# One attention-and-experts kernel: two gathers, one set of transposes and four row tiles change their place

## The chip, the cores and the metric

The kernel runs on one NeuronCore of a Trainium2 chip, as one program with one launch. The metric is device time in microseconds (us). Before the change the median of three runs is 446.9 us (446.38 to 448.73).

The engines that matter here: TensorE (PE in the profile, its weight loads PEld), VectorE (DVE), ScalarE (ACT), GpSimd (POOL) and SyncE (SP), which issues most of the transfers. Each engine works through its own instructions in order; semaphores tie them together.

## The reference, cut to what matters

Two blocks follow each other. The first is a linear attention with decay over 4 sequences (B), 8 heads of 64 (H, D) and 768 positions, cut in blocks of 64:

```python
intra = np.einsum('bhic,bhjc->bhij', qb, kb) * Dmask[None]      # scores, decayed and causal
intra = np.einsum('bhij,bhjd->bhid', intra, vb)
inter = np.einsum('bhid,bhde->bhie', qb * lam_pow[None], kv_state)
out[:, :, sl] = intra + inter
kv_state = lam_block * kv_state + np.einsum('bhsd,bhse->bhde', kb * rev_pow[None], vb)
```

Its output, 3072 rows of 512 numbers, goes through a mixture of 8 experts. Each row takes the expert with the highest logit, or keeps the expert of the row before it where a local gate says so:

```python
fresh_e = int(np.argmax(logits[b, s]))
e = fresh_e if s == 0 or local_gate[b, s] < 0.5 else prev_e
h = np.maximum(x[b, s] @ w1[e], 0.0)
out[b, s] = p[e] * (h @ w2[e])
```

## The kernel before

**Attention, 24 steps.** The kernel takes blocks of 128 positions instead of 64. A step `s` is one block of 128 positions of one sequence (`ORDER`, line 33): the four sequences take turns, so steps 0 to 3 are the first blocks of the four, 4 to 7 the second blocks, and so on. Steps 20 to 23 are the last blocks, which update no state. In one step:

- `loaded` brings queries, keys and values of a step in by SP (1 MB; 0.75 MB for the last four), five steps ahead.
- `prepare` lets POOL multiply the queries by the decay powers (`qd`, line 178, "decayed queries") and the keys by theirs (`kd`, line 181), three steps ahead.
- `scores(s + 1)` is the product of keys and queries in PSUM (`ps`, lines 201 and 209), and DVE multiplies it by the decay mask into `sm` (line 213). For steps in `WIDE` it is 8 matmuls of 128 columns and all positions; otherwise it is 16 matmuls on quarters of the array, which leave the half above the diagonal out. (A float32 matmul is two records in the trace, so these are x16 and x32 there.) There is one pair of `ps` tiles, so the next scores wait until DVE has read the last.
- `from_state` (line 236) is the product of state and decayed queries, `mix` (line 249) adds scores times values into the same PSUM tile `po`, and ACT copies the result into `xc` (line 252). `xc` holds one step of each sequence.
- `update` (line 263) brings the state forward; DVE adds it (line 266).

**Rows out.** The output of a step is held turned, and must be turned back into rows for `x_dram`, from where the experts gather rows. This happens in one of two ways. `rows_of` uses four PE transposes (line 273), an ACT copy (line 278) and one transfer of 256 KB, which ACT's queue issues (line 282). For steps in `TURNED`, `turned_rows` uses one DVE transpose (line 294), and after the last step of a group of four, `group_out` sends four transfers by SP (line 302). `TURNED[r]` is the step in which row tile `r` is turned. Before, these are steps 0 to 11 (mostly one step later) and 20 to 22.

**Routing, between the steps.** `gates` and `logits` take the logits of four steps. `extras` (line 793) spreads the routing of the first 12 tiles of rows over steps 9 to 22, most of it on DVE: `fresh_experts`, `along_sequences`, `experts_of`, `ranks`, `first_tiles`, `tokens_to_first_tiles`, `brought`, `by_slots`. It ends at (19, 1) with `gidx` (line 650), the row indices. At (20, 0) POOL issues the first two gathers, `ahead(0, 0)` and `ahead(1, 1)` (line 725), of 128 rows each, into `xgt[0]` and `xgt[1]`.

**The first expert tile.** `first_turned` (lines 732 to 735) transposes `xgt[0]` on PE into `pr` and lets DVE copy it to `xtt[0]`. The first product of the experts, `hidden(0, 0, 0)` (line 753), reads it directly after step 23.

**Experts.** 5 whole tiles are worked through while the rest of the routing is done, then pairs of tiles, whole tiles and half tiles as the counts need. Weights come by SP (lines 701 to 709, 831 to 837), 2 MB each.

**Order.** PE, DVE, SP and POOL follow the order in which the program is written (`manual_schedule`, line 807); only ACT is ordered by the scheduler. Ahead of the change, within step `s`, the order is: `loaded`, `prepare(s + 3)`, weight loads, `scores(s + 1)`, `from_state(s)`, logits, extras, gates, `mix(s)`, `update(s)`, `first_turned` in step 23, rows out, late extras.

Of the kernel before, what the change touches and what calls it, by code (L numbers as in the profile page):

```python
# [38 lines left out]
PARTS = [(0, 8), (8, NA), (NA, NT)]  # L39
LOADS = 6  # L40
QUARTERS = [16, 17, 18, 19]
WIDE = [3, 4, 5, 7, 9, 11]
TURNED = {**{r: r + 1 for r in range(3 * B)}, 11: 13, 20: 22, 21: 23, 22: 23}
WARM = 10
KA = -(-(NA * P - E * (P - 1)) // P)

# [19 lines left out]
def kernel(  # L66
# [120 lines left out]
    def scores(s):  # L187
        x = inp[s]
        qt = x[:, 0].rearrange("p (a i) -> p a i", i=P)
        kt = x[:, 1].rearrange("p (a i) -> p a i", i=P)  # L190
        if s == 1:
            ps = [t.rearrange("p (a i) -> p a i", i=P) for t in (pl, pr)]
        else:
            ps = pss


        if s in WIDE:
            for a in range(A):
                for u in range(2):
                    rows = slice(DH * u, DH * u + DH)  # L200
                    nc.tensor.matmul(ps[u][:, a], lhsT=kt[rows, a], rhs=qt[rows, a],
                                     start=True, stop=True, skip_group_check=True)
        for a in range(A if s not in WIDE else 0):
            for j in range(2):
                first = DH * j if s > 1 else 0
                half = slice(DH * (j ^ a & 1), DH * (j ^ a & 1) + DH)
                for u in range(2):
                    rows = slice(DH * u, DH * u + DH)
                    nc.tensor.matmul(ps[u][half, a, first:], lhsT=kt[rows, a, half], rhs=qt[rows, a, first:],  # L209
                                     start=True, stop=True, skip_group_check=True)  # L210
        sm = sms[s] = att.tile([P, 2, A, P], F32, name="sm")
        for u in range(2):
            nc.vector.tensor_tensor(sm[:, u], ps[u], mask[:, u], ALU.mult)  # L213
# [14 lines left out]
    def from_state(s):  # L228
        b, c = ORDER[s]
        head = heads[s] = place_of(s)  # L230
        if c:
            kv, qd = kvs[b], qds.pop(s)
            for a in range(A):
                for u in range(2):
                    rows = slice(DH * u, DH * u + DH)
                    nc.tensor.matmul(head(a, u), lhsT=kv[rows, a], rhs=qd[rows, a],  # L236
                                     start=(a < 2), stop=False, skip_group_check=True)
            if c + 1 < NC:
                for a in range(A):
                    nc.scalar.mul(kv[:, a], kv[:, a], lamq[:, a, P - 1:P])  # L240
# [491 lines left out]
    def first_turned():  # L732
        for d in range(DT):
            nc.tensor.transpose(pr[:, P * d:P * d + P], xgt[0][:, P * d:P * d + P], ident)
        nc.vector.tensor_copy(xtt[0].rearrange("p d i -> p (d i)"), pr)  # L735
# [67 lines left out]
    def extra_work(s, k):  # L803
        if (s, k) in extras:
            extras[s, k]()

    with tc.manual_schedule(engines={PE, DVE, SP, POOL}):

        warm = pg.tile([P, A, P], F32, name="pk0")
        for _ in range(WARM):  # L810
            nc.tensor.matmul(warm[:, 0], lhsT=ident, rhs=ident, start=True, stop=True)
        masks_of_lam()
        nc.gpsimd.memset(wgt, 0.0)
        constants_1()

        for s in range(LOADS - 1):
            inp[s] = load.tile([P, 4, DM], F32, name="inp")
        for s, half in ((0, 0), (1, 0), (0, 1), (1, 1), *((s, half) for s in range(2, LOADS - 1) for half in range(2))):
            nc.sync.dma_start(out=inp[s][:, 2 * half:2 * half + 2], in_=qkv[s][:, 2 * half:2 * half + 2])
        for s in range(3):  # L820
            prepare(s)
        scores(0)
        nc.sync.dma_start(out=wgt[:, :, :E + 1], in_=wg)
        for s in range(NS):
            if s + LOADS - 1 < NS:
                loaded(s + LOADS - 1)
            if s + 3 < NS and s != 1:
                prepare(s + 3)
            if s in QUARTERS:
                j = QUARTERS.index(s)  # L830
                nc.sync.dma_start(out=w1t[0][:, j], in_=w1_src(0)[:, j])
            if s == NS - 4:
                nc.sync.dma_start(out=w2t[0], in_=w2_src(0))
                weights(0)
            if s == NS - 1:
                nc.sync.dma_start(out=w1t[1], in_=w1_src(1))
                nc.sync.dma_start(out=w2t[1], in_=w2_src(1))
            if s + 1 < NS and s not in (1, 2, 3, 4, 5):
                scores(s + 1)
            from_state(s)  # L840
            if s % B == 1 and s > B:
                logits(s // B - 1)
            if s == 5:
                scores(6)
            extra_work(s, 0)
            if s % B == 0 and s:
                gates(s // B - 1)
            mix(s)
            if s == 0:
                update(0)  # L850
                query_powers(0)
            if s in (1, 2, 3, 4):
                scores(s + 1)
            if s == 1:
                query_powers(1)
                prepare(4)
            if s:
                update(s)
            if s + 1 == NS:
                first_turned()  # L860
            if s > 1 and s - 1 not in TURNED:
                rows_of(s - 1)
            for r in [r for r in TURNED if TURNED[r] == s]:
                turned_rows(r)
                if r + 1 not in TURNED or r % B == B - 1:
                    group_out(r // B)
            extra_work(s, 1)
        x_ctx.close()
        act = ctx.enter_context(tc.tile_pool(name="act", bufs=2))
        w1t.append(act.tile([P, DT, F], F32, name="w1_2", bufs=1))  # L870
        w2t.append(act.tile([P, FT, DM], F32, name="w2_2", bufs=1))
        pools.append(act)

        pys.extend(pg.tile([P, DM], F32, name=f"pk{i}") for i in range(2))
        hq.update({(f, 1): act.tile([P, FT // 2, P], F32, name=f"h{f}1", bufs=1) for f in range(2)})
        xgh = act.tile([P, DM], F32, name="xgh", bufs=1)
        yt = act.tile([P, 2, DM], F32, name="y", bufs=1)
        xps = [act.tile([P, DT, P], F32, name=f"xp{i}", bufs=1) for i in range(3)]
        xs = act.tile([P, 3, DT // 2, P], F32, name="xs", bufs=1)
        s1 = act.tile([P, 3, DT // 2, F // 2], F32, name="s1", bufs=1)  # L880
        yl = s1[:, 0]
        s2 = act.tile([P, 3, FT // 2, DM // 2], F32, name="s2", bufs=1)
        hs = act.tile([P, 4, FT // 2, P], F32, name="hsum", bufs=1)
        part = act.tile([P, 3, FT // 2, P], F32, name="part", bufs=1)
        rest = act.tile([P, DM // 2], F32, name="rest", bufs=1)

        def finished(g):
            output(g % 2, g % 2)
            written(g, g % 2)

        def hiddens(g):
            hidden(g % 2, g % 2, 0)
            hidden(g % 2, g % 2, 1)


        xqs.extend((xlast, rt.tile([P, DM], F32, name="lg")))
        ahead(2, 0)
        xq = hq[1, 0].rearrange("p f i -> p (f i)")
        flipped(xq, xgt[1])
        ahead(3, 1)  # L900
        moved(xtt[1], xq, (0, 1))
        hidden(0, 0, 0)
        rows_of(NS - 1)
        weights(1)
        gates(NC - 1)
        moved(xtt[1], xq, (2, 3))
        hidden(0, 0, 1)
        by_slots(0, (2, 3, 4))
        logits(NC - 1)
        fresh_experts(2)  # L910
        flipped(xqs[1], xgt[0])
        ahead(4, 0)
        moved(xtt[0], xqs[1])
        finished(0)
        weights(2)
        along_sequences(2)
        flipped(xqs[0], xgt[1])
        hiddens(1)
        moved(xtt[1], xqs[0])
        experts_of(2)  # L920
        chances(2)
        flipped(xqs[1], xgt[0])
        finished(1)
        weights(3)
        ranks(2)
        masks(2)
        other_tiles()
        tokens_to_other_tiles()
        hiddens(2)
        moved(xtt[0], xqs[1])  # L930
        output(0, 0)
        weights(4)
        brought(1, (0, 1, 2, 3, 4))
        written(2, 0)
        hiddens(3)
        weights_of(KA, w_of(0), (1,))
        output(1, 1, range(FT // 2))
        by_slots(1, (0, 1, 2, 3, 4))
        output(1, 1, range(FT // 2, FT))
        written(3, 1)  # L940
# [417 lines left out]
```

## Time and profile before

| what | us |
|---|---|
| median of three runs | 446.9 |
| the profiled execution, its time | 447.0 |
| its span (first to last instruction) | 445.3 |
| PE busy in the span | 427.9 |
| DVE busy | 286.4 |
| ACT busy | 195.0 |
| POOL busy | 108.7 |
| attention, up to the start of the first expert product | 100.13 |

A "span" is what the trace shows from the program's first instruction to its last; the time of the profiled execution is 1.7 us longer. Times within the trace count from the start of the span. In lists of instructions, a line gives start, duration, engine, line of the kernel, operation, tiles, shapes and count, and in brackets the engine's idle time before it and what ended it.

### The profile page before, as it was taken

What the parts mean: (1) busy time and instruction counts of PE and PEld (TensorE: products, weight loads), DVE (VectorE), ACT (ScalarE), POOL (GpSimd) and SP (SyncE); (2) the same over time, 40 slices, a digit from 0 to 9 for tenths busy, and PEclk for the clock granted to TensorE, in tenths of its full rate; (3) what the DMA queues carried; (4) which work ended last, traced back from release to release, by engine and by line L of the source; (5) the groups of instructions that cost most, each with busy time, mean ns of one, the idle gap of its engine ahead of it and who ended that gap; (6) DMA issues with size and microseconds to landing.
All of it is one profiled execution on the core that took longest, in us unless ns stands there. A gap on an engine that the chain in (4) does not pass through costs nothing.

```text
span 445.3 us, 10336 instructions
## 1 busy us (share of the span) xinstructions
PE 427.9 (96%) x4094; PEld 354.9 (80%) x4094; DVE 286.4 (64%) x564; ACT 195.0 (44%) x592; POOL 108.7 (24%) x120
## 2 busy tenths in 40 slices
PE   6999989889999999999999999999999999999993
PEld 6787777678667876978777999667899999898982
DVE  5767986882339949757372785100587879878661
ACT  4245555436455104663234456451455454565110
POOL 4495574321100042205121301200202021020101
PEclk9999999899999999999999999999999999999998
DMA  8999999979999899999993799996164828370101
GB/s 265 409 366 384 369 327 330 348 292 370 345 401 364 277 306 394 399 396 405 393 399 144 236 399 370 326 380 223 40 214 138 311 84 300 131 268 3 54 1 52
DMA packets 48352, 124.84 MB, mean 280 GB/s; under 512 B 3165, under 2 KB 10845, under 8 KB 46369
## 3 DMA queue, kind: packets, MB, share of 16 engines
q1 hardware_dynamic: 42624, 108.03, 66.5%
q0 software_dynamic: 4368, 13.90, 8.8%
q10 hardware_dynamic: 1296, 2.10, 1.3%
q8 instruction: 36, 0.59, 0.5%
q14 instruction: 28, 0.22, 0.2%
HBM read 124.02 MB, written 12.91 MB: 308 GB/s over the span
## 4 chain that ended last, share of the span: by engine, by line
PE 76%; DMA 11%; issue 6%; DVE 5%; POOLq 0%; POOL 0%; ACT 0%; DVEq 0%
PE ps L753 13%; PE pk L759 12%; PE ps L981 11%; PE pk L986 10%; DMA out_dram<-y,sidxp 6%; PE po L249 5%; PE po L981 5%; PE pl L986 4%; DMA w<-in_w_dram 4%; PE ps L209 3%; PE po L236 2%; PE pr L1142 2%; DVE sm L213 2%; PE pk L263 2%; PE pl L308 2%
## 5 line engine op out<-in xcount | busy, mean ns | idle before, releaser
L753 PEld LDWEIGHTS ps<-xt,w 128*128 128x128 f32 x512 | 58.2, 192 | 3.5 <-issue 2.3
L753 PE MATMUL ps<-xt,w 128*128 128x128 f32 x512 | 59.1, 276 | 0.8 <-DVE xt L735 0.8
L759 PE MATMUL pk<-w,h 128*128 128x512 f32 x128 | 56.5, 593 | 0.0
L759 PEld LDWEIGHTS pk<-w,h 128*128 128x128 f32 x128 | 23.6, 190 | 26.3 <-issue 25.6
L768 POOL DMA_INDIRECT out_dram<-y,sidx x14 | 14.0, 1001 | 105.4 <-DVE y L785 46.5
L725 POOL DMA_INDIRECT xg<-x_dram,gidx x25 | 25.8, 1031 | 55.5 <-DVE lg L739 34.1
L746 ACT COPY xp<-xlast 32x128 f32<-32x128 f32 x128 | 37.8, 295 | 1.7
L213 DVE TENSOR_TENSOR sm<-ps,mask 128x512 f32<-128x512 f32 x46 | 29.5, 682 | 9.6 <-PE ps L209 4.9
L755 ACT ACTIVATE h<-ps 128x512 f32<-128x512 f32 x16 | 9.6, 597 | 56.3 <-PE ps L753 56.3
L746 ACT COPY xp<-lg 32x128 f32<-32x128 f32 x112 | 33.0, 295 | 2.6
L785 DVE TENSOR_SCALAR y<-pk,gate 128x512 f32<-128x512 f32 x8 | 6.0, 744 | 42.1 <-PE pk L759 25.8
L178 POOL TENSOR_TENSOR qd<-inp,lamq 128x512 f32<-128x512 f32 x20 | 25.5, 1276 | 28.8 <-DMA inp<-in_qkv_dram 18.3
L981 PEld LDWEIGHTS ps<-xp,w 128*128 128x128 f32 x256 | 30.4, 192 | 2.1 <-issue 1.8
L981 PE MATMUL ps<-xp,w 128*128 128x128 f32 x256 | 31.4, 276 | 0.1
L981 PE MATMUL ps<-xs,s 128*128 128x128 f32 x256 | 31.2, 275 | 0.0
L986 PE MATMUL pk<-w,h 128*128 128x256 f32 x128 | 30.5, 381 | 0.0
L986 PE MATMUL pk<-s,hsum 128*128 128x256 f32 x128 | 30.3, 380 | 0.0
L249 PE MATMUL po<-sm,inp 128*64 128x128 f32 x384 | 28.0, 283 | 2.3 <-DVE sm L213 1.6
L249 PEld LDWEIGHTS po<-sm,inp 128*64 128x64 f32 x384 | 21.5, 139 | 10.6 <-issue 6.4
L981 PEld LDWEIGHTS ps<-xs,s 128*128 128x128 f32 x256 | 29.9, 192 | 0.0
L986 PEld LDWEIGHTS pk<-s,hsum 128*128 128x128 f32 x128 | 23.9, 190 | 3.3 <-DVE s L1069 0.2
L986 PEld LDWEIGHTS pk<-w,h 128*128 128x128 f32 x128 | 23.5, 190 | 3.4 <-issue 0.6
(282 smaller groups left out, 784.4 us busy)
## 6 DMA issues: line engine op xcount, KB each, us to landing
w<-in_w_dram SPq DMA_DIRECT2D x43, 2048.0 KB, 12.8
inp<-in_qkv_dram SPq DMA_DIRECT2D x15, 1024.0 KB, 10.9
inp<-in_qkv_dram SPq DMA_DIRECT2D x10, 512.0 KB, 7.9
x_dram<-w SPq DMA_DIRECT2D x12, 256.0 KB, 6.3
inp<-in_qkv_dram SPq DMA_DIRECT2D x4, 768.0 KB, 9.2
x_dram<-xn ACTq DMA_DIRECT2D x8, 256.0 KB, 6.7
w<-in_w_dram SPq DMA_DIRECT2D x4, 512.0 KB, 5.7
x_dram<-inp SPq DMA_DIRECT2D x4, 192.0 KB, 10.4
```

The lines of the kernel that those rows point to most:

```text
L178: nc.gpsimd.tensor_tensor(qd, x[:, 0].rearrange("p (a i) -> p a i", i=P), lamq, ALU.mult)
L209: nc.tensor.matmul(ps[u][half, a, first:], lhsT=kt[rows, a, half], rhs=qt[rows, a, first:], start=True, stop=True, skip_group_check=True)
L213: nc.vector.tensor_tensor(sm[:, u], ps[u], mask[:, u], ALU.mult)
L249: nc.tensor.matmul(head(a, u), lhsT=vn[:, a, u], rhs=sm[:, u, a], start=(not c and a < 2), stop=True, skip_group_check=True)
L725: nc.gpsimd.indirect_dma_start(out=xg, out_offset=None, in_=x_dram[:n, :], in_offset=bass.IndirectOffsetOnAxis(ap=gidx[i][:, j:j + 1], axi ...
L746: copy(xt[QP * j:QP * j + QP, :, QP * k:QP * k + QP], blocks[QP * k:QP * k + QP, :, j])
L753: nc.tensor.matmul(ph[:, j], lhsT=w1t[w][:, d, P * f:P * f + P], rhs=xtt[i][:, d], start=(d == 0), stop=(d == DT - 1))
L755: nc.scalar.activation(hq[half, i], ph, ACT.Relu)
L759: nc.tensor.matmul(pys[i], lhsT=hq[f // 4, i][:, f % 4], rhs=w2t[w][:, f], start=(f == 0), stop=(f == FT - 1))
L768: apart(nc.gpsimd.indirect_dma_start(out=out, out_offset=bass.IndirectOffsetOnAxis(ap=sidx[i][:, j:j + 1], axis=0), in_=y, in_offset=None, ...
L981: nc.tensor.matmul(to[:, m], lhsT=a[:, k, P * m:P * m + P], rhs=b[:, k], start=(new and not m and not k), stop=(k == 1), skip_group_check= ...
L986: nc.tensor.matmul(to, lhsT=a[:, f], rhs=b[:, f], start=(new and not f), stop=(f == FT // 2 - 1), skip_group_check=True)
```

## The change

The diff:

```diff
-WIDE = [3, 4, 5, 7, 9, 11]
-TURNED = {**{r: r + 1 for r in range(3 * B)}, 11: 13, 20: 22, 21: 23, 22: 23}
+WIDE = [3, 4, 5, 7, 9, 11, 13]
+TURNED = {**{r: r + 1 for r in range(4 * B)}, 11: 13, 12: 15, 13: 15, 20: 22, 21: 23, 22: 23}
...
-            if s + 3 < NS and s != 1:
+            if s + 4 < NS and s != 1:
                 prepare(s + 3)
...
             if s + 1 < NS and s not in (1, 2, 3, 4, 5):
                 scores(s + 1)
+            if s + 1 == NS:
+                first_turned()
             from_state(s)
             if s % B == 1 and s > B:
                 logits(s // B - 1)
             if s == 5:
                 scores(6)
             extra_work(s, 0)
+            if s + 4 == NS:
+                prepare(NS - 1)
...
             if s:
                 update(s)
-            if s + 1 == NS:
-                first_turned()
```

- The row tiles of steps 12 to 15 go from `rows_of` to `turned_rows`. Tiles 12, 13 and 14 are turned at the end of step 15, tile 15 at the end of step 16, after which `group_out(3)` sends all four by SP.
- The scores of step 13 are made in the wide form.
- `prepare(23)`, which makes the last decayed queries, stands behind the first two gathers in POOL's order instead of ahead of them.
- `first_turned` stands at the start of step 23, ahead of `from_state(23)`, instead of behind `mix(23)`.

## The prediction, as it went on record

> **What bounds the kernel now.** I read the chain of waits first. It runs through PE without a break from 100.13 us, where the first expert product starts, to 387 us. Behind 100 us PE waits once, for 0.54 us at 217.88. The change touches nothing there, so its worth is read at one point: when does `hidden(0, 0, 0)` start? Next I read VectorE's instructions in order of time, from step 15 on:
>
> ```profile
> 64.83 1.29 DVE L213 TENSOR_TENSOR sm<-ps,mask 128x512 f32<-128x512 f32 x2 [0.24 <-PE ps L209]
> 66.04 0.18 DVE L451 TENSOR_TENSOR hot<-pr,down 128x32 bf16<-128x32 f32 x1
> 66.92 0.42 DVE L266 TENSOR_TENSOR kv<-pk,kv 128x256 f32<-128x256 f32 x1 [0.70 <-PE pk L263]
> 68.28 1.29 DVE L213 TENSOR_TENSOR sm<-ps,mask 128x512 f32<-128x512 f32 x2 [0.94 <-PE ps L209]
> 69.71 0.24 DVE L469 TENSOR_TENSOR_SCAN incl<-go,tot 128x40 f32<-128x40 bf16 x1
> ...
> 71.33 0.42 DVE L266 TENSOR_TENSOR kv<-pk,kv 128x256 f32<-128x256 f32 x1 [0.34 <-PE pk L263]
> 73.60 0.69 DVE L213 TENSOR_TENSOR sm<-ps,mask 128x512 f32<-128x512 f32 x1 [1.84 <-PE ps L209]
> ...
> 86.76 1.29 DVE L213 TENSOR_TENSOR sm<-ps,mask 128x512 f32<-128x512 f32 x2 [0.90 <-PE ps L209]
> ```
>
> The brackets are the point. From 64.6 to 73.6 DVE waits for PE: 0.24 + 0.70 + 0.94 + 0.14 + 0.34 + 1.84 = 4.2 us. From 73.60 to 85.86 it has no wait over 0.15 us, then one of 0.90, and then from 86.76 to 98.5 it is full but for two short waits on ACT. So PE sets the pace up to step 17 and DVE from there to the end. The third view is the last step:
>
> ```profile
> 95.46 1.09 PE L249 MATMUL po<-sm,inp 128*64 128x128 f32 x16
> 96.90 0.84 PE L236 MATMUL po<-qd,kv 64*64 64x128 f32 x16 [0.34 <-ACT xc L252]
> 97.67 1.09 PE L249 MATMUL po<-sm,inp 128*64 128x128 f32 x16
> 98.69 0.66 PE L734 MATMUL pr<-ident,xg 128*128 128x128 f32 x4
> 100.13 0.38 PE L753 MATMUL ps<-xt,w 128*128 128x128 f32 x1 [0.78 <-DVE xt L735]
> ```
>
> `mix(23)` waits for the last `sm` (96.22 to 97.50 on DVE). Transposes and a DVE copy (99.38 to 100.07) then stand between it and the experts.
>
> **Part 1: rows 12 to 15 to VectorE.** Each `rows_of` leaves PE: four transposes, 0.59 us a set in the chain of waits (4 x 0.59 = 2.36). ACT loses four copies of 0.585 and four issues of 0.33, which lay beside PE. DVE gains four transposes of 0.70; two back to back took 1.29, so three take about 1.98 and the sum is 2.68, all at the ends of steps 15 and 16. That is inside the stretch with 4.2 us of waits. DVE can start `sm(18)` (now 73.60) at most 4.2 - 2.68 = 1.5 us earlier. Can PE follow? It sheds 2.36, less what part 2 costs, 0.5: 1.86 us, enough. So DVE decides and I take **-1.5**. The bounds: -1.86, if DVE has more room than I count; 0, if DVE's new work only replaces its waits.
>
> From `sm(18)` on DVE is the bound, so the 1.5 us reach `gidx` (85.86), and the work up to the last `sm` unless PE comes late. The 0.90 wait ahead of `sm(21)` comes from PE's own stall:
>
> ```profile
> 86.09 0.60 PE L209 MATMUL ps<-inp 64*64 64x64 f32 x18 [1.24 <-issue]
> ```
>
> PE waited for nothing that the profile shows. Such stalls end at PE's matmul records 1100 (1.27 us), 1352 (0.65) and 1604 (1.24), 252 records apart, each 1.2 to 1.5 us after a 16 KB packet on the instruction queue has ended. So code arrives late at fixed places of the instruction stream. The change takes 16 records out ahead of them by part 2 and 16 by part 1, so the third moves by 32 records, from inside `scores(21)` to the end of `from_state(20)`. There it no longer holds `sm(21)`, and up to `sm(22)`, which DVE reaches 5.5 us behind `sm(21)` (86.76, 92.28), PE has 2 us of room: in that stretch it lost 1.24 + 1.34 us (stall and slow clock, below) and was still in time. But a stall could also stay ahead of `sm(21)`, if fewer records count than I think. Between -0.90 and 0 I take **-0.9**, since 32 records are more than the 18 that `scores(21)` has left at the stall.
>
> [...]
>
> SP gains `group_out(3)` in step 16, ahead of the loads for steps 22 and 23. Its first transfer waits for row 15, turned at about 72 us; a group takes SP 3.9 to 4.2 us to issue (27.09, 40.94, 60.30). The load for step 22 can thus go at about 76.3, and it goes at 75.92 now, since the weight load ahead of it waits 8.2 us for an ACT row write, as the waits of SP show:
>
> ```profile
> SPq L831 <- DMA x_dram<-xn: 14.1, 3, 8.2
> ```
>
> Cost 0, hidden by 6 to 7 us: the step-22 data land at about 84.3 (the POOL multiply starts on them at 84.37) and `scores(22)` starts at 91.31; the step-23 data about 88.1 and 94.19. Without that cover, each us of delay is a us of `scores`.
>
> **Part 2: wide scores of step 13.** Unhindered, a wide set lasts 1.09 us (23.70 to 24.79) and a narrow one 0.72 (63.87 to 64.59). Where both wait for DVE's last `sm`, the following `from_state` starts 1.08 after the release for the wide one (35.39 to 36.47) and 0.58 for the narrow one (50.53 to 51.11): **+0.5** on PE, taken in part 1. DVE's `sm` starts as early in both (0.98 and 0.96 after the release).
>
> **Part 3: gathers ahead of the last queries.** POOL now holds them behind a multiply that waits for the step-23 load:
>
> ```profile
> 88.15 1.27 POOL L178 TENSOR_TENSOR qd<-inp,lamq 128x512 f32<-128x512 f32 x1 [2.51 <-DMA inp<-in_qkv_dram]
> 89.58 1.21 POOL L725 DMA_INDIRECT xg<-x_dram,gidx  x1 [0.17 <-DVE kd L498]
> 91.10 1.01 POOL L725 DMA_INDIRECT xg<-x_dram,gidx  x1 [0.31 <-issue]
> ```
>
> The first gather can start at `gidx`, 85.86, which is 3.7 us earlier. The second landed at 97.75, 6.65 after its start; the same for the first gives 92.5. Queued behind them is only the multiply: now at about 88.2, done by 89.5, wanted by `from_state(23)` at 96.90. Nothing is gained by itself, but part 4 needs it. Taken at 0; if the first gather lands after the transposes come up (96.55), it costs 1:1 beyond some 0.5 us.
>
> **Part 4: transposes first.** On today's clock `mix(22)` ends at 96.55 and PE idles 0.34 for ACT; the transposes go there (to 97.21), `from_state(23)` starts 0.3 later and ends about 97.8, and `mix(23)` ends at 98.8, as now. DVE copies behind `val` and row 20 (ending 98.52): 98.52 + 0.69 = 99.21, product at 99.27 instead of 100.13. **-0.86**. The two rows behind the copy and the flip of `xgt[1]` also come 0.8 earlier. Bounds: 0 if the gather is late by 1.4, -1.3 if nothing but `mix(23)` held the product.
>
> **Sum.** -1.5 - 0.9 - 0.86 = -3.3 us on the profiled execution's own time, 447.0 (span 445.3 and 1.7 around it; the median of the runs is 446.9): **443.7**. Does it survive the experts? From 146 to 162 us the DMA share is 0.70 to 0.94, and the weight issues of the long full stretch after it (161.88 to 205.57) are each released by PE, so they move along.
>
> **Rivals.**
> (a) DVE gives all of part 1 back: its new 2.68 us are not covered, since the waits are places where PE needs `sm` and the transposes stand ahead of it. For it: DVE is full from 73.6 on. Against: 4.2 us of waits. Left is part 4: 447.0 - 0.86 = 446.1.
> (b) A stall for code, or a half clock, falls on the path. The profile shows one such clock:
>
> ```profile
> 85.00:90.00 5.00, 3.91 (x51) 1.91 (x52) 3.71 (x8) 0.40 (x2) 2.32 (x3) 0.68 1.02 404
> 90.00:95.00 5.00, 5.00 (x120) 4.15 (x120) 4.22 (x20) 2.39 (x7) 1.80 (x2) 0.98 1.05 397
> ```
>
> The third number from the end is the granted clock: half speed from 86.81 to 90.22, behind the 1.24 us stall; the gates took 1.94 instead of 1.06 and `mix(20)` 1.55 instead of 1.09, 1.34 together. With PE idling for DVE in steps 18 and 19, another dip is possible. On the path: 443.7 + 1.24 + 1.34 = 446.3.
> [...]
> (c) Slower: SP's queue. `group_out(3)` and the weight loads behind it each wait for earlier transfers to land, as the 8.2 us did. If the step-22 load goes only when a group transfer has landed (76.3 + 6.3, the median landing of those) and the step-23 load after another such 6.3, at 88.9, then its data land 9.5 later, at 98.4, where `scores(23)` starts at 94.19 now: +4.2 - 0.86 = 450.3. It decides from where the step-23 data land later than about 91 (94.19 less the 3.3); it makes a loss from about 95. For it: earlier landings do block SP now. Against: the change takes away the ACT writes that block it.
>
> **Chances.** Forecast 0.62 (its own range 442.9 to 444.9), (a) 0.14, (b) 0.12, (c) 0.12. About 0.5%, 2.2 us, is what a measurement of this kernel tells from no change; the line is at 444.7. Nearly all of the forecast lies below: faster 0.60. Slower is (c): 0.12. The rest is same: 0.28. The range takes in (a) and (b) and leaves out (c) and a little more: from all bounds together, 447.0 - 1.86 - 0.90 - 1.3 = 442.9, to (b), 446.3, each widened by the 0.5 that the fastest run lies below the median (446.38, 446.9): 442.4 to 446.8.
>
> **What would show it.** `sm(18)` at about 72.1, `sm(21)` straight behind line 650; no long DVE wait from 66 to its end; the PE stalls elsewhere; the first gather near 84 to 86; transposes ahead of line 236 in step 23; the first line 753 product at 96.9. Wrong if `sm(18)` stays at 73.6, if line 734 waits for a gather, or if lines 209 wait for loads.

## The result

The changed kernel is slower: 448.85 us (median of 21 runs, 445.53 to 451.27) against 446.64 us (21 runs beside them, 444.47 to 448.73), a ratio of 1.005 with a 95% interval of 1.0031 to 1.0069. In a second batch, unchanged, it gave 447.47 us against 445.61 us, 1.0027 (0.9998 to 1.0056). The forecast was 443.7 us, in a range up to 446.8. Ratios and intervals here and below are over fast runs and can differ from the quotient of the two medians.

The profiled execution took 449.19 us, with a span of 447.4 us (445.3 before). Three starts on PE and the end of the span show where the difference arises:

| event | before | after | difference |
|---|---|---|---|
| first expert product | 100.13 | 101.27 | +1.14 |
| second tile's first product | 117.01 | 119.56 | +2.55 |
| third tile's first product | 131.56 | 134.08 | +2.52 |
| end of the span | 445.3 | 447.4 | +2.1 |

So two losses are to be explained: 1.1 us where 3.3 us were to be gained in the attention, and 1.4 us more between the first and the second expert tile, a place that the prediction never looked at. Behind it the kernels run alike, but for the wait of 0.54 us at 217.88 us, which is gone.

First the attention. VectorE's instructions in order of time, after, in the same columns as before:

```profile
68.91 1.89 DVE L294 STREAM_TRANSPOSE w<-xc 128x512 f32<-128x512 f32 x3
70.72 1.25 DVE L213 TENSOR_TENSOR sm<-ps,mask 128x512 f32<-128x512 f32 x2
...
73.40 0.70 DVE L294 STREAM_TRANSPOSE w<-xc 128x512 f32<-128x512 f32 x1
74.03 1.25 DVE L213 TENSOR_TENSOR sm<-ps,mask 128x512 f32<-128x512 f32 x2
...
86.48 1.29 DVE L213 TENSOR_TENSOR sm<-ps,mask 128x512 f32<-128x512 f32 x2 [0.28 <-PE ps L209]
...
94.19 1.29 DVE L213 TENSOR_TENSOR sm<-ps,mask 128x512 f32<-128x512 f32 x2 [3.31 <-PE ps L209]
```

The four transposes are there, 1.89 + 0.70 = 2.6 us, and of the 4.2 us of waits around them 0.75 are left (ahead of line 266 at 68.57). But `sm(18)` starts at 74.03, not at 72.1, and ahead of `sm(22)` DVE waits 3.31 us for PE, where it waited for nothing before. PE's own instructions show why:

```profile
88.70 0.43 PE L236 MATMUL po<-qd,kv 64*64 64x128 f32 x3 [1.84 <-issue]
...
90.06 1.74 PE L249 MATMUL po<-sm,inp 128*64 128x128 f32 x16
91.73 1.12 PE L273 MATMUL pk<-ident,xc 128*128 128x128 f32 x4
92.78 1.34 PE L209 MATMUL ps<-inp 64*64 64x128 f32 x32
...
98.46 0.66 PE L734 MATMUL pr<-ident,xg 128*128 128x128 f32 x4
99.04 0.67 PE L236 MATMUL po<-qd,kv 64*64 64x128 f32 x16
99.64 1.13 PE L249 MATMUL po<-sm,inp 128*64 128x128 f32 x16
101.27 0.94 PE L753 MATMUL ps<-xt,w 128*128 128x128 f32 x6 [0.50 <-DVE xt L735]
```

PE's stall did move from `scores(21)` to the end of `from_state(20)`. It took 1.84 us there instead of 1.24, and the half clock (granted clock 0.50 from 90.35 to 93.76) came behind it: `mix(20)` took 1.74 us, the four row transposes 1.12 and the scores 1.34, against 1.09, 0.66 and 0.90 at the full clock; by the starts of these lines that is 1.6 us more. The last four lines show part 4 as it was meant: transposes ahead of the state product, and the first product 1.64 us behind the end of the last `sm` (99.63), where it was 2.63.

Now the second loss. PE, at the second tile:

```profile
117.89 0.33 PE L433 MATMUL pr<-identb,each 128*4 128x128 bf16 x3
119.56 7.38 PE L753 MATMUL ps<-xt,w 128*128 128x128 f32 x64 [1.34 <-DMA w<-in_w_dram]
```

It waits 1.34 us for weights. The transfers that SP's queue sent ahead of that point, after (columns: start and duration of the issue, engine, line, operation, tiles, count):

```profile
74.13 3.74 SPq L302 DMA_DIRECT2D x_dram<-w  x4
80.34 0.35 SPq L171 DMA_DIRECT2D inp<-in_qkv_dram  x1
80.90 0.35 SPq L831 DMA_DIRECT2D w<-in_w_dram  x1
88.55 0.33 SPq L171 DMA_DIRECT2D inp<-in_qkv_dram  x1
...
89.87 0.64 SPq L833 DMA_DIRECT2D w<-in_w_dram  x1
98.70 0.10 SPq L701 DMA_DIRECT2D w<-in_w_dram  x1
104.72 0.08 SPq L702 DMA_DIRECT2D w<-in_w_dram  x1
104.85 0.39 SPq L836 DMA_DIRECT2D w<-in_w_dram  x1
...
105.90 9.06 SPq L302 DMA_DIRECT2D x_dram<-inp  x4
115.07 3.51 SPq L282 DMA_DIRECT2D x_dram<-xlast  x1
119.34 0.09 SPq L701 DMA_DIRECT2D w<-in_w_dram  x1
```

and the end of the same list before:

```profile
85.29 0.47 SPq L833 DMA_DIRECT2D w<-in_w_dram  x1
91.64 0.10 SPq L701 DMA_DIRECT2D w<-in_w_dram  x1
98.83 0.08 SPq L702 DMA_DIRECT2D w<-in_w_dram  x1
98.96 0.39 SPq L836 DMA_DIRECT2D w<-in_w_dram  x1
...
101.32 10.16 SPq L302 DMA_DIRECT2D x_dram<-inp  x4
111.57 1.26 SPq L282 DMA_DIRECT2D x_dram<-xlast  x1
113.98 0.09 SPq L701 DMA_DIRECT2D w<-in_w_dram  x1
```

The last line is the conditional weight load of the second tile (`weights(1)`). In the profiled execution nothing is loaded by it, but PE started only when SP had passed it: 119.34 is 0.22 us ahead of PE's 119.56. Before, SP passed it at 113.98, 3.0 us ahead of PE. From the top of the list, one delay is handed down: `group_out(3)` at 74.13, the load of step 22 at 80.34 (75.92 before), that of step 23 at 88.55 (78.65), `w2t[0]` at 89.87 (85.29), then the conditional load of the second half of the first tile's weights (line 702), which stands still until `w2t[0]` has landed (104.72 against 98.83), and behind that the last rows. The four issues of the group take 3.74 us; most of the 9.9 us at step 23 comes from a landing. SP's waits show 2.3 us ahead of the load of step 22 for a weight quarter, and 7.2 us ahead of that of step 23 for a row write of ACT's queue:

```profile
SPq L171 <- DMA x_dram<-xn: 7.2, 1, 7.2
```

### The profile page after: what moved, and what is told of

Its sections match the earlier page's. It is cut to its first block, busy times and chain, and to the rows that moved or that the text cites. A ratio compares the mean times of both kernels' runs of the same rounds, so it can differ in the third digit from the quotient of the medians.

```text
span 447.4 us, 10298 instructions
## 1 busy us (share of the span) xinstructions
PE 426.9 (95%) x4062; PEld 355.1 (79%) x4062; DVE 288.8 (65%) x568; ACT 192.9 (43%) x588; POOL 109.3 (24%) x120
## 4 chain that ended last, share of the span: by engine, by line
PE 58%; DMA 6%; issue 5%; DVE 2%; POOLq 0%; POOL 0%; DVEq 0%
PE ps L753 11%; PE ps L983 11%; PE pk L988 11%; PE pk L759 11%; DMA out_dram<-y,sidxp 6%; PE po L983 5%; PE pl L988 4%; PE pr L1144 2%; PE pr L1122 2%; DVE s L962 1%; PE pr L641 0%; PE po L1112 0%; DVE w L963 0%; POOLq L1356 0%; DVE s L963 0%
## 5 line engine op out<-in xcount | busy, mean ns | idle before, releaser
L249 PE MATMUL po<-sm,inp 128*64 128x128 f32 x384 | 28.9, 287 | 3.2 <-DVE sm L213 1.6
```

The lines of the kernel that those rows point to most:

```text
L249: nc.tensor.matmul(head(a, u), lhsT=vn[:, a, u], rhs=sm[:, u, a], start=(not c and a < 2), stop=True, skip_group_check=True)
```

## The experiments

**Theories.** Q: SP's queue. `group_out(3)` delays everything behind it up to `weights(1)`, and PE pays at the second tile. F: fetching of code; the stalls fall on worse places, with the half clock behind them. V: VectorE gives part 1 back. Every median below stands beside that of the kernel before in the same batch; "first product" and "second tile" are starts in the one profiled execution.

### The parts alone

tail_alone keeps parts 3 and 4 and has `WIDE` and `TURNED` as before; rows_alone is the kernel before with the new `TURNED` only.

```diff
 tail_alone (against after)
-WIDE = [3, 4, 5, 7, 9, 11, 13]
-TURNED = {**{r: r + 1 for r in range(4 * B)}, 11: 13, 12: 15, 13: 15, 20: 22, 21: 23, 22: 23}
+WIDE = [3, 4, 5, 7, 9, 11]
+TURNED = {**{r: r + 1 for r in range(3 * B)}, 11: 13, 20: 22, 21: 23, 22: 23}
 rows_alone (against before)
-TURNED = {**{r: r + 1 for r in range(3 * B)}, 11: 13, 20: 22, 21: 23, 22: 23}
+TURNED = {**{r: r + 1 for r in range(4 * B)}, 11: 13, 12: 15, 13: 15, 20: 22, 21: 23, 22: 23}
```

> The two gathers and the transposes are moved, rows 12 to 15 and the scores of step 13 stay as before. Theory F (the loss of the change comes from PE's code stalls, shifted by 32 records, and from the half clock behind them): the records ahead of step 23 are those of before, so nothing is shifted and only the tail's 0.9 us is won, about 445.7. Theory Q (the loss comes from the fourth group's transfers in SP's queue): SP's order is that of before, so also -0.9. Theory R (the tail's move itself is bad, the gather arrives late): no gain, line 734 or what follows waits.

> Only rows 12 to 15 go to VectorE; scores of step 13 narrow, gathers and transposes as before. F: 16 records fewer instead of 32, so the third stall falls in another place, late in scores(21); the loss is smaller or gone, 445.5 to 447. Q: the SP order is that of the change, the weights of the second tile are asked for about 5 us late, PE waits at the second tile's first product (line 753) for about 1.3 us, total about 448 to 449.5.

tail_alone: 445.69 against 446.71 us, 0.9983 (0.9961 to 1.0006); first product 98.54, second tile 115.42, no wait. rows_alone: 452.31, 1.0103 (1.0061 to 1.0145); first product 103.54, second tile 122.99. The loss comes with the row tiles and not with the tail. In rows_alone it is larger than in the changed kernel, and POOL's instructions say why:

```profile
92.97 1.27 POOL L178 TENSOR_TENSOR qd<-inp,lamq 128x512 f32<-128x512 f32 x1 [7.38 <-DMA inp<-in_qkv_dram]
94.41 1.21 POOL L725 DMA_INDIRECT xg<-x_dram,gidx  x1 [0.16 <-DVE kd L498]
```

With the late load of step 23 the last multiply stands 7.38 us, and the first gather, still behind it, leaves at 94.41. PE's transposes then wait for the gather:

```profile
101.87 0.89 PE L734 MATMUL pr<-ident,xg 128*128 128x128 f32 x4 [2.20 <-DMA xg<-x_dram,gidx]
```

Behind this wait the transposes took 0.89 us, against 0.66 in the changed kernel, and the first product 6.41 us instead of 3.84. The wait expected at the second tile did not come: PE got there at 122.99, 4.1 us after SP had passed line 701 (118.91). Part 3, costed at nothing, is thus what keeps the gathers (87.83 in the changed kernel) out of the delay that part 1 causes in SP's queue.

### The queue of SP

Six kernels change only who sends a transfer, or its place in SP's order. Three edits are shown; act_w1_early has those of rows_by_act and w1_early together, before_w1_early that of w1_early in the kernel before, and tail_w1_early the same in tail_alone.

```diff
 rows_by_act
-            nc.sync.dma_start(
+            (nc.scalar if k == 3 else nc.sync).dma_start(
 group_late
-                if r + 1 not in TURNED or r % B == B - 1:
+                if (r + 1 not in TURNED or r % B == B - 1) and r // B != 3:
                     group_out(r // B)
+            if s == 18:
+                group_out(3)
 w1_early
             if s == NS - 4:
                 nc.sync.dma_start(out=w2t[0], in_=w2_src(0))
+                nc.sync.dma_start(out=w1t[1], in_=w1_src(1))
                 weights(0)
             if s == NS - 1:
-                nc.sync.dma_start(out=w1t[1], in_=w1_src(1))
```

> The whole change, but the four transfers of the fourth group are issued from ACT's queue. Q: the loads of steps 22 and 23 leave SP by about 79 again, the weights of the second tile are asked for near 99 instead of 104.85, no wait for weights at line 753: 1.3 to 2 us under the changed kernel, about 447. F: the instruction stream of PE is that of the changed kernel, its stall near from_state(20) stays, first expert product about 101, total still 448 or more.

> The whole change, but group_out(3) stands at the end of step 18 in SP's order, behind the loads of steps 22 and 23 and the weight quarters j0 to j2, instead of in step 16. Q: these loads no longer stand behind the four transfers; the load of step 23 leaves by about 79, w2t[0] by about 85, w1t[1] by about 100, no wait of over 0.8 us at the second tile; total 446 to 447. F: PE's instructions are those of the changed kernel; if the code stall in from_state(20) (1.84) and the half clock behind it are the cause by themselves, the first expert product stays at about 101 and the total at 448 to 449.

> The whole change, but the load of w1t[1] stands ahead of the conditional weights of tile 0 in SP's order, so it does not wait for w2t[0] to land. Q, last link: the wait at the second tile's first product (1.34) is gone though the loads before it are as late as in the changed kernel; total 1 to 1.5 under the changed kernel, 447.3 to 448. F: the first product stays at about 101 in both theories. If the wait is paid for by something else later (w2t[1] of the same tile, then the next tile's weights), the total stays near 448.8.

> Group 3 by ACT's queue and w1t[1] ahead: if rows_by_act (446.19) was held by the 0.75 us wait at the second tile, this takes it: 445.4 to 445.8, and the first product near 97.4. If the transfer ahead of the gathers delays them, line 734 waits and the gain is lost, 446 to 447.

> The kernel before, with only the load of w1t[1] ahead of the conditional weights of tile 0. Control for w1_early: Q says that this load is on the path only in the changed kernel, so here it does nothing: within 0.5 of before, no wait at line 753. If it wins 1 us or more here, w1_early's gain is a gain of its own and says nothing of the change.

> Gathers and transposes moved, rows 12 to 15 as before, w1t[1] early. If the tail alone is worth 0.9 and nothing waits for weights: 445.2 to 445.9, like tail_alone (445.69). If tail_alone was partly held by the second tile's weights, up to 0.7 better.

| kernel | median, us | before | ratio (95%) | first product | second tile | its wait |
|---|---|---|---|---|---|---|
| rows_by_act | 446.19 | 446.71 | 0.9997 (0.9970 to 1.0023) | 97.36 | 115.06 | 0.75 |
| group_late | 446.39 | 446.28 | 1.0005 (0.9972 to 1.0038) | 98.24 | 117.39 | 2.21 |
| w1_early | 445.29 | 446.28 | 0.9996 (0.9974 to 1.0018) | 98.40 | 115.28 | none |
| act_w1_early | 446.23 | 446.28 | 1.0007 (0.9984 to 1.0030) | 99.56 | 116.44 | none |
| before_w1_early | 446.22 | 445.61 | 1.0013 (0.9996 to 1.0030) | 99.72 | 116.59 | none |
| tail_w1_early | 445.46 | 445.61 | 0.9989 (0.9969 to 1.0009) | 99.73 | 116.61 | none |

w1_early leaves `group_out(3)` where the change put it and all work as it was; it only keeps one load of 2 MB from standing behind the conditional load. SP, in w1_early:

```profile
88.11 0.68 SPq L833 DMA_DIRECT2D w<-in_w_dram  x1
89.26 4.25 SPq L834 DMA_DIRECT2D w<-in_w_dram  x1
...
110.59 2.62 SPq L282 DMA_DIRECT2D x_dram<-xlast  x1
114.17 0.09 SPq L701 DMA_DIRECT2D w<-in_w_dram  x1
```

and PE:

```profile
115.02 0.33 PE L433 MATMUL pr<-identb,each 128*4 128x128 bf16 x3
115.28 7.41 PE L753 MATMUL ps<-xt,w 128*128 128x128 f32 x64
```

Line 701 goes at 114.17, 5.2 us earlier than in the changed kernel, the wait is gone, and with it the loss: 0.9996 (0.9974 to 1.0018) against 1.0050 (1.0031 to 1.0069) of the changed kernel; only the interval of its repetition (0.9998 to 1.0056) overlaps a little. The same edit gains nothing in the kernel before, nor in the tail alone, where the wait does not occur. That is Q. The gain was larger than expected (1 to 1.5 us, with the first product near 101): the attention ended at 98.40, which this edit doesn't explain. Four profiles with the same work up to there (after, after_again, and weights_first and filler below) have 101.27, 99.89, 98.74 and 98.38, so it differs from one execution to the next. Q is not the whole of it either: w1_early is only level with before, and 98.40 is still behind the forecast's 96.9. The load of step 23 left at 86.79 here, as late as in the changed kernel.

rows_by_act shows the other half. It takes the four transfers out of SP's queue (loads of steps 22 and 23 at 78.36 and 79.34), and the attention ends at 97.36; but ACT now stands for 4.39 us:

```profile
70.85 4.39 ACTq L302 DMA_DIRECT2D x_dram<-w  x4
75.34 1.06 ACT L240 ACTIVATE kv<-kv,lamq 128x64 f32<-128x64 f32 x4 [5.99 <-DVE ends L537]
```

The four issues of the group held ACT for 4.39 us here, as they held SP for 3.74 in the changed kernel, and PE waited 2.69 us for ACT's copy `xc`. group_late keeps the loads of steps 22 and 23 in time (71.31, 75.25), but the group goes at 84.06, ahead of `w2t[0]` (90.05), and the wait at the second tile is 2.21 us, against an expected 0.8 at most. act_w1_early fell short too, 446.23 and 99.56 where 445.4 to 445.8 and 97.4 were expected: PE again waited 2.69 us for ACT.

### Queue order, landing or clock?

weights_first moves the last rows behind `weights(1)` in SP's order; filler puts 16 identity matmuls, whose result nothing reads, ahead of the second tile's first product, so that PE doesn't idle in the wait; after_again is the changed kernel again.

```diff
 weights_first
-                if r + 1 not in TURNED or r % B == B - 1:
+                if (r + 1 not in TURNED or r % B == B - 1) and r // B != 5:
                     group_out(r // B)
...
         weights(1)
+        group_out(5)
 filler
+        if i == 1 and not half and not filled:
+            filled.append(1)
+            for _ in range(16):
+                nc.tensor.matmul(ph[:, 0], lhsT=ident, rhs=ident, start=True, stop=True)
```

> The changed kernel itself once more, beside the next three on one chip, for a comparison without a change of chip. All theories: 448 to 449.5, 2 us over before. Q: a wait of 1 to 4 us at the second tile's first product, released by SP's conditional weight load (line 701), which leaves near 119.

> The whole change, but the four transfers of the last group of rows (20 to 22) stand in SP's order behind the conditional weights of the second tile instead of ahead of them. The load of w1t[1] leaves as late as in the changed kernel (near 104.5). If SP's queue is what PE waits for, the conditional load (line 701, 119.15 to 119.34 in the changed kernel) leaves by 113 to 116, the wait at the second tile falls to under 0.5 us and the total to 445.5 to 446.5. If the landing of w1t[1] is what it waits for, 15 us after its issue, the wait stays at 1.5 to 2.5 us and the total at 447.5 to 449.

> The whole change, with 16 matmuls of the identity (32 records, about 2 us of PE) ahead of the second tile's first product, where PE waits 1.3 to 2.5 us for SP. They leave no product out and change no result; they only keep PE busy in the wait. If the half clock behind the wait (120.78 in the repeat of the changed kernel; tile 2 to tile 3 took 16.15 us instead of 14.5) comes from the idle, it goes: 14.5 us between these tiles and a total of 446 to 447, in spite of added work. If it has another cause, it stays, and the total is 447.5 to 449.5.

after_again, PE:

```profile
119.36 9.01 PE L753 MATMUL ps<-xt,w 128*128 128x128 f32 x64 [2.52 <-DMA w<-in_w_dram]
```

Here the attention ended at 99.89, 1.4 earlier than in the first profile, and the second tile starts at the same time, 119.36: SP decides it. The product takes 9.01 us instead of 7.38, since from 120.78 the clock was halved for 3.4 us (a mean granted clock of 0.66 from 120 to 125). In this execution another 1.6 us thus came behind the wait of 2.52.

weights_first: 451.96 against 445.62 us, 1.0138 (1.0094 to 1.0181). The wait at the second tile is gone (SP passed line 701 at 112.48, PE started at 115.62), although `w1t[1]` was sent at 104.59, as late as in the changed kernel: PE had waited for SP's queue and not for the data. The total rose because of what was put back. PE's next product then waits:

```profile
127.26 0.24 PE L449 MATMUL pr<-identb,run 4*128 4x4 bf16 x3 [4.23 <-DVE run L442]
```

The conditional load of line 702 held SP until 118.53 and the last rows went behind it, at 118.67. Their issues ended at 121.3. DVE's line 785 writes a tile that is laid out only when the attention's tiles are given up; it stood 14.00 us and started at 124.96. So the order is a bind: rows first delays PE by the weights, weights first delays it by the rows.

filler: 449.32, 1.0072 (1.0046 to 1.0098). PE:

```profile
115.23 3.84 PE L755 MATMUL ps<-ident 128*128 128x128 f32 x32
119.01 7.41 PE L759 MATMUL ps<-xt,w 128*128 128x128 f32 x64
```

SP passed line 701 at 118.89, so the product started when SP allowed it, as in the changed kernel (119.56 and 119.36), although the attention had ended at 98.38. The filler hid a wait that would have been as long as itself, 3.8 us, and the total stayed where the other branch of the expectation had it. No half clock followed (granted clock 1.00 from 115 to 130) and the product took 7.41 us. That fits idling as its cause, but doesn't show it: none followed the waits of 1.34 us in the first profile and 2.21 in group_late either.

### Code and the wide form

warm_26 moves every matmul record behind the warm-up by 32; narrow_13 takes part 2 back.

```diff
-WARM = 10
+WARM = 26
 narrow_13
-WIDE = [3, 4, 5, 7, 9, 11, 13]
+WIDE = [3, 4, 5, 7, 9, 11]
```

> The whole change with 16 more warm-up matmuls at the start (32 more records), while PE waits for the first data anyway; this moves the borders of the code blocks back by 32 records against the work, to where they lay before from step 17 on. F: the 1.8 us stall in from_state(20) moves into scores(21) as before; the time changes by 1 to 2 us against the changed kernel, likely down to about 447. Q: SP's queue is unchanged, the late weights and the 1.3 us wait at the second tile stay, total within 0.5 of the changed kernel's 448.85 (plus anything that the longer warm-up costs at the start).

> The whole change without the wide scores of step 13, so 16 records fewer are shifted. F: the stalls move by 16 records, the third goes back towards scores(21); the time may move by 1 us either way, between 447.5 and 450. Q: SP's order is that of the change, the weights stay late, total within 0.7 of 448.85. The 0.5 us that the wide form costs on PE is hidden in both.

warm_26: 453.59 against 446.71 us, 1.0118 (1.0075 to 1.0161). The longer warm-up put the first scores 5.0 us later (10.83, in the changed kernel 5.83) and the third `mix` still 3.3 (17.51 and 14.22), so the total says nothing on F. narrow_13: 449.25 against 446.28, 1.0065 (1.0035 to 1.0095), which cannot be told from the changed kernel; the 0.5 us of part 2 remain unmeasured. Both again waited at the second tile, 3.94 and 3.34 us.

### The two edits together

late_w1_early joins group_late and w1_early; late_w1_again repeats it; late_w1_first also moves the last rows behind `weights(1)`.

> The whole change, group_out(3) at the end of step 18 and w1t[1] early. group_late still had a wait of 2.2 us at the second tile (w1t[1] left at 102.75) with the first product at 98.2. Q: both together take the wait away and keep the earlier product: 444.5 to 445.5, the best version so far. F: with the wait gone, what remains above 444 are code stalls and half clocks, whose places differ from run to run.

> The best version once more on this chip: 1.0 to 2.0 us under before (ratio 0.9955 to 0.998). If 444.07 was luck of the chip or of the places of the code stalls, 445.5 or more.

> The best version, and the last group of rows behind the conditional weights of the second tile too. The best version's profile shows no wait at the second tile, so nothing more is on the path there: equal to late_w1_again within 0.5. If in part of its runs the wait is still there, up to 0.7 better.

late_w1_early: 444.07 against 445.61 us, 0.9981 (0.9955 to 1.0007). late_w1_again: 443.77 against 445.62, 0.9957 (0.9932 to 0.9981). PE, in late_w1_again:

```profile
96.95 3.84 PE L753 MATMUL ps<-xt,w 128*128 128x128 f32 x32 [0.50 <-DVE xt L735]
...
113.57 0.33 PE L433 MATMUL pr<-identb,each 128*4 128x128 bf16 x3
113.83 7.41 PE L753 MATMUL ps<-xt,w 128*128 128x128 f32 x64
```

The first product is at 96.95 (96.63 in the first of the two), the wait is gone, and the kernel beats both others: late_w1_again has the only interval of all that lies below 1, while that of late_w1_early reaches past it. late_w1_first: 445.01, 0.9996 (0.9966 to 1.0026), 1.2 us over late_w1_again where 0.5 at most was expected; PE waits 1.31 us for `run` at 122.23, a small form of the bind above.

## Why the prediction was wrong, by its steps

**The step that failed** is the paragraph on SP in part 1: "Cost 0, hidden by 6 to 7 us". It took the cover from the kernel before, in which the data of step 23 land at about 88.1 and `scores(23)` starts at 94.19. But the load left at 88.55 instead of 78.65, and the forecast itself wanted `scores(23)` 3.3 us earlier, at about 90.9. POOL's multiply, which starts on these data, started at 94.68, 93.30, 92.53, 93.77 and 92.15 in after, after_again, w1_early, filler and weights_first. So the cover was gone. In most of these profiles PE shows no wait for the load only because `scores(23)` came later still (96.10 in the first one). In filler it shows one:

```profile
93.74 0.90 PE L209 MATMUL ps<-inp 64*64 64x128 f32 x32 [1.31 <-DVE parts L507]
93.77 1.26 POOL L178 TENSOR_TENSOR qd<-inp,lamq 128x512 f32<-128x512 f32 x1 [4.02 <-DMA inp<-in_qkv_dram]
```

The bracket names a VectorE instruction whose result the scores don't read; the scores and the multiply start together, on the same data. Even there `sm(23)` didn't wait (95.38, VectorE was full), so that these loads cost the kernel time by `scores` is not shown.

What is shown is the cost of what the same step left out, everything behind these two loads: the weight quarters, `w2t[0]`, two conditional loads, `w1t[1]` and the last rows, and at the end a load for which PE waits, with 3.0 us of cover (113.98 to 117.01). Against a PE that comes 3.3 us earlier that cover is gone even if SP loses nothing; with line 701 going 5.4 us later, PE had to wait.

**The test of the sum against the experts** failed with it: "the weight issues of the long full stretch after it (161.88 to 205.57) are each released by PE, so they move along". That looked behind the place. The claim "Behind 100 us PE waits once" was true of before, and says nothing on how close the next waits are. The worth was to be read at two points, the first product and the second tile.

**Rival (c)** named this queue and `scores(23)`, sent the load at 88.9 (88.55 measured) and said that it decides from where the data land later than about 91, as they did. It was held unlikely because "the change takes away the ACT writes that block it". It doesn't: steps 16 to 19 keep `rows_of`, and one of their row writes held the load for 7.2 us. The match of the time is in part luck, since (c) had the group's own transfers in the place of that write and of the weight quarter. Its victim was not the one that paid: no profile shows `sm(23)` waiting for the scores, and the second tile isn't named.

**Part 1 on VectorE** was right in its mechanism, and V falls: four transposes, 2.6 us, went into 4.2 us of waits. The size varies. `sm(18)` started at 74.03 and 72.20 in the two profiles of the changed kernel, at 70.74 in rows_by_act and at 70.60 and 70.64 in the two of the best version, against 73.60 before and 72.1 predicted. In the first profile 1.8 us went in step 13, where two DVE instructions of 0.27 and 0.19 us before lay beside POOL's multiplies:

```profile
58.53 1.30 DVE L422 TENSOR_TENSOR top<-lt,mx 128x32 f32<-128x32 f32 x1
59.87 0.97 DVE L423 TENSOR_TENSOR top<-top,down 128x32 f32<-128x32 f32 x1
```

```profile
58.51 1.27 POOL L178 TENSOR_TENSOR qd<-inp,lamq 128x512 f32<-128x512 f32 x1 [0.22 <-DMA inp<-in_qkv_dram]
59.75 1.04 POOL L181 TENSOR_TENSOR kd<-inp,rev 128x512 f32<-128x512 f32 x1
```

Each of the two DVE instructions ends within 0.05 us of a POOL multiply (59.83 and 59.78, 60.84 and 60.79).

**The stall** moved as counted, off `sm(21)` (86.48, 0.28 of wait) to the end of `from_state(20)`. The "2 us of room" before `sm(22)` were not there: PE lost 1.84 us by the stall and 1.6 by the slow clock, and DVE waited 3.31. Two readings were off. The stall of 1.24 us before ended at 86.09, ahead of `sm(21)`, so the old profile had shown room for 1.34 only, and not for both. And DVE was ready for `sm(22)` at 90.88, 4.4 us behind `sm(21)` instead of 5.5, since its line 664 took 0.17 us instead of 1.27. In that profile rival (b) happened as well. But it doesn't decide the kernel: late_w1_early had stalls of 1.11, 1.01 and 0.58 us at the same records and still reached 96.63, and w1_early, with 1.43 and 1.30, lost nothing to before.

**Parts 3 and 4** were right. The product came 1.64 us behind the last `sm` (1.77 predicted, 2.63 before), and tail_alone's 1.0 us is near the 0.86, though its interval reaches past 1, and tail_w1_early gained only 0.15 by its median.

**The sum** came out in the attention where the loads of steps 22 and 23 left early and PE stood for nothing else: the first product was at 96.63 and 96.95 in the best version and 96.63 in late_w1_first, 96.9 predicted. In rows_by_act, act_w1_early and group_late, where these loads left by 81.2 too, PE stood 2.69, 2.69 and 2.02 us for ACT or DVE, and it was at 97.36, 99.56 and 98.24. The terms divide otherwise than predicted: in the best version `sm(18)` came 3.0 us earlier instead of 1.5, but `sm(21)` 2.3 to 2.6, where 1.5 + 0.9 = 2.4 were predicted. So the two terms ahead of `sm(21)` came out in their sum only, which is in part luck. How the late loads hold the attention back elsewhere is open but for one link: POOL's multiply on the data of step 23 then runs beside VectorE's work between `sm(22)` and `sm(23)`, which took 4.2 to 4.9 us in after, after_again, w1_early, filler and weights_first, and 3.9 in the best version.

That 443.77 and 444.07 us stand so near the predicted 443.7 is luck as well. The kernel before took 445.6 in these batches, so the best version gains 1.5 to 1.9 us and not 3.3. Counted so, the change cost 2.2 and 1.9 us where 3.3 were to be gained, and the two edits in SP's order gave 3.4 to 4.1 of these 5.2 to 5.5 us back. How that divides, in a given execution, between the attention, the wait at the second tile (1.34 to 3.94 us), and the half clock behind it (1.6, in after_again and narrow_13) was not separated. Where the rest of the predicted gain went is open.

## What to carry to other kernels

Price a transfer that is put into a queue by everything that stands behind it up to the first instruction that another engine waits for, and not by the next two loads; the cover that counts is the smallest on the whole way, taken at the time at which the waiting engine will be there after the gain. A gain upstream uses up cover downstream: list how far ahead of its user each transfer comes, before counting on it. A skipped conditional load was not free in SP's queue: line 702 stood 5.5 us in the changed kernel until the load into the tile that it would write had landed, so an unconditional load goes ahead of it here.

## What the runs showed of the hardware

- In the changed kernel the load of step 23 stood until 88.55 for a row write of ACT's queue (7.2 us in SP's waits), with which it shares no data. The write left at 81.44 and landed 7.0 us later. Why the load waits for it is open.
- The granted clock was 0.50 from 86.81 to 90.22 in the kernel before, and from 63.04 to 66.45 and 90.35 to 93.76 in the changed kernel, 3.41 us each. PE had idled 1.24, 1.83 and 1.84 us shortly ahead of these (up to 86.09, 62.32 and 88.70). The length of a gap doesn't decide by itself. Behind 2.52 us in after_again and 3.34 in narrow_13 the product took 9.01 us; behind 1.34 in the changed kernel (granted clock 1.00 from 119 to 122) and 2.21 in group_late it took 7.38, and behind 2.69 in rows_by_act the next `mix` took 1.09, as at the full clock. What orders them is open. In a full stretch the half clock cost 1.6 us (9.01 against 7.41).
- In the changed kernel, its repetition and the two of the best version, PE's stalls between 72 and 89 us, for which the profile names no releaser, fell on the same instructions but differed in length. The one in line 236, in `from_state(20)`, took 1.84 us in the changed kernel, 1.14 in its repetition, and 0.58 and nothing in the two of the best version; the one in line 249 took 0.84, 0.57, 1.11 and 0.57, and the one in line 209 took 0.91, nothing, 1.01 and nothing. In the changed kernel's first profile they ended 1.3 to 1.6 us after a 16 KB packet on the instruction queue, at 74.19, 80.85 and 87.36. That fits code that comes late; no view shows what PE waits for.
